# Six tile buffers, earlier token sums and later residual adds in a two-layer spectral and dense kernel

## The chip, the cores and the metric

The kernel runs on one core of one Trainium2 chip, as one launch. The metric is the device time of the whole launch in microseconds (us), the median of several runs.

The engines are named as in the profile: PE is TensorE (matmul), DVE is VectorE, ACT is ScalarE, POOL is GpSimd, and SP is the queue that issues most DMAs. Each engine works through its own list of instructions in order; a wait at the head of a list holds everything behind it.

## What is computed

The input x has 2048 tokens of 1024 features. Two kinds of layer follow each other, twice:

```
x = x + A(layernorm(x))      # A: 2-D real FFT, times a complex filter, inverse FFT
x = x + B(layernorm(x))      # B: Mish(x @ w1 + b1) @ w2,  w1 1024x3584, w2 3584x1024
x = x + A(layernorm(x))
x = x + B(layernorm(x))
```

Both A layers share their filter and both B layers share w1, b1 and w2. The change concerns the two B layers only.

## The kernel before

A B layer handles the 2048 tokens as four chunks of 512 (chunk 0 to 3), each of four tiles of 128 tokens. A tile j (0 to 15) is a 128 x 1024 slice of the resident array XS. The steps of one B layer, in the order in which `layer_B` writes them:

1. **First chunks.** Tiles 0 to 7 get statistics, scale and `apply` (line 521, normalises a tile into a buffer XN), are transposed on PE (line 1108) and copied by DVE (line 1113) into XT. `mm1` (line 1141) multiplies six groups of w1 columns directly. `residual(j)` (line 1284) adds the staged result of the A layer to XS for tiles 4 to 15; the adds for tiles 8 to 11 stand ahead of the normalisation of tiles 6 and 7. Statistics of tiles 8 to 15 come later.
2. **First quads.** `quads` multiplies the remaining eight column groups for chunks 0 and 1 together, in a Strassen-Winograd form of seven products (`product`, line 1177) of four matmuls each per group. It needs sums of the transposed tokens. `open_pair` makes them with four DVE subtractions of 128 x 2048 (line 1156): T1, T2, T4 in three tiles TS0 to TS2 at 128 to 140 KB, and T3 over a part of XT. The first sum reads both chunks. `quads` calls `open_pair` before its first product.
3. **Second product.** Loop n = 0 to 15: `mm2` (line 1228, 28 matmuls of 128 x 512 over all of the hidden features) makes half of the output of one of tiles 0 to 7. It uses PSUM banks 3, 4, 5 in turn, and DVE adds the bank to XS (line 1240). n below 8 makes the first halves, n from 8 the second. In the same loop, for n below 8, `apply(8 + n)` normalises a tile of chunk 2 or 3 into one of two XN buffers, and `turned` issues eight DMA transposes (line 250) from it, all on SP. A buffer is used again two tiles later, when its eight transposes have landed. In the first B layer each `mm2` is followed on DVE by statistics of its half, and from n = 8 also by the scale and `apply` of the finished tile for the next layer: a tail of ten instructions.
4. **Second quads.** `quads` runs over all 14 column groups for chunks 2 and 3, with its own `open_pair` first. Its first group of products is A11 B11, S2 T2, S1 T1, A12 B21, S3 T3, in that order on PE. DVE adds the result of S2 T2 (`add(u2, ...)`, line 1182) before S3 T3 may go into the same bank, then adds S3 T3 (`add(u3, ...)`).
5. **Last second product.** 16 calls of `mm2` for tiles 8 to 15.

The order on every engine is the order of the code. The list of DVE in step 3, for one n, is `apply` of tile 8 + n, then the add of product n. PE can run ahead of the adds by three products, one in each bank.

Of the kernel before, what the change touches and what calls it, by code (L numbers as in the profile page):

```python
# [180 lines left out]
class KB:  # L181
# [183 lines left out]
    def layout(self):  # L365
        K = 1024
        self.o = dict(XR=0, Z=0, X=12 * K, T=20 * K, YK=28 * K, V=40 * K, JT=48 * K, M0=49 * K, IDF=49 * K + 256, RT=50 * K,
                      JUNK=51 * K, WR=54 * K, YS=96 * K, UT=64 * K, MN=64 * K, Y=96 * K, XN=128 * K, U=128 * K,
                      FT=140 * K, BT=144 * K + 512, WT=self.W1_OFF)
        self.ob = dict(AT0=0, AT1=36 * K, XT1=28 * K, XT0=120 * K, W2=64 * K, JUNK=54 * K, SUMS=92 * K, TS=128 * K, XN2=140 * K,  # L370
                       WS=self.arena_bytes - 21 * K)
        assert 149 * K <= self.W1_OFF and 144 * K <= self.ob["WS"], (149 * K, self.W1_OFF)

# [714 lines left out]
    def layer_B(self, li, last):  # L1088
# [60 lines left out]
        def open_pair():  # L1149

            T = [self.alloc(f"TS{i}", self.ob["TS"] + 4096 * i, [4, 512], F16) for i in range(3)]
            lo, hi = [[XT[c].ap[:, 4 * k:4 * k + 4, :] for c in range(2)] for k in range(2)]
            t3 = lo[1].bitcast(F16)
            both = r_xt[0] + r_xt[1]
            tt = lambda dst, x, y, reads, writes: self.op(
                dve, lambda e: e.tensor_tensor(dst, x, y, ALU.subtract), reads=reads, writes=writes)  # L1156
            tt(T[0].ap, lo[1], lo[0], both, [T[0].res])
            tt(T[1].ap, hi[1], T[0].ap, both + [T[0].res], [T[1].res])
            tt(T[2].ap, hi[0], T[1].ap, both + [T[1].res], [T[2].res])
            tt(t3, hi[1], lo[1], r_xt[0], r_xt[1])  # L1160
            return {"B11": (lo[0], r_xt[0]), "B21": (hi[0], r_xt[0]), "B22": (hi[1], r_xt[1]), "T3": (t3, r_xt[1]),
                    "T1": (T[0].ap, [T[0].res]), "T2": (T[1].ap, [T[1].res]), "T4": (T[2].ap, [T[2].res])}

        def open_sums():

            off = self.ob["SUMS"]
            return [self.alloc(f"SUM{i}", off + 2048 * i, [512], F32) for i in range(5)]

        def quads(fgs, slot_of, after=lambda n: None):

            B, sums = open_pair(), open_sums()

            def product(n, bank, a, b, start):
                s = slot_of[n]
                A = self.wblock(s, a)
                mov, res = B[b]
                self.group([lambda e, db=db: e.matmul(PS[:, bank, :], A[:, db, :], mov[:, db, :], start=(start and db == 0), stop=(db == 3),  # L1177
                                                      skip_group_check=True)
                            for db in range(4)], reads=[s.res, s.rs] + list(res), writes=[self.r_bank[bank]])

            def add(dst, bank, x):
                self.op(dve, lambda e: e.tensor_tensor(dst.ap, PS[:, bank, :], x.ap, ALU.add), reads=[self.r_bank[bank], x.res],  # L1182
                        writes=[dst.res])

            def mish(c, ft, src, res):
                at, ra = AT[c], r_at[c][ft]
                self.op(act, lambda e: e.activation(at.ap[:, ft, :], src, ACT.Mish, bias=self.B1[:, ft:ft + 1]),  # L1187
                        reads=[res, self.r_b1], writes=[ra])

            def parts(n):  # L1190
                a, b, d = (3 * (n % 2) + i for i in range(3))
                return a, b, d, sums[n % 2], sums[2 + n % 2], sums[4], 2 * fgs[n]

            N = len(fgs)
            for n in range(N + 1):
                if n < N:
                    a, b, d, p1, u2, u3, ft = parts(n)
                    product(n, a, "A11", "B11", True)
                    self.copy(act, p1.ap, PS[:, a, :], [self.r_bank[a]], [p1.res])
                    product(n, b, "S2", "T2", True)  # L1200
                    add(u2, b, p1)
                if n:
                    _, pb, pd, q1, q2, q3, pft = parts(n - 1)
                    mish(1, pft + 1, q3.ap, q3.res)
                    product(n - 1, pb, "A22", "T4", False)
                    add(q1, pb, q1)
                    mish(0, pft + 1, q1.ap, q1.res)
                    product(n - 1, pd, "S4", "B22", False)
                    add(q2, pd, q2)
                    mish(1, pft, q2.ap, q2.res)  # L1210
                    after(n - 1)
                if n < N:
                    product(n, d, "S1", "T1", True)
                    product(n, a, "A12", "B21", False)
                    mish(0, ft, PS[:, a, :], self.r_bank[a])
                    product(n, b, "S3", "T3", False)
                    add(u3, b, p1)
                    add(u3, d, u3)

        def mm2(c, t, h):  # L1220
            at, ra = AT[c % 2], r_at[c % 2]
            j = 4 * c + t
            bank = 3 + no[0] % 3
            no[0] += 1
            fns = []
            summed = not last and (j, h) == (15, 1)
            for i, ft in enumerate(range(NF)):
                fns.append(lambda e, i=i, ft=ft: e.matmul(  # L1228
                    PS[:, bank, :], at.ap[:, ft, t * P:(t + 1) * P], W2[h][ft // 4].ap[:, ft % 4, :],
                    start=(i == 0), stop=(i == NF - 1 and not summed)))  # L1230

            for lo, hi in ((0, 20), (20, NF)):
                self.group(fns[lo:hi], reads=ra[lo:hi] + [b.res for b in W2[h][lo // 4:hi // 4]], writes=[self.r_bank[bank]])
            if summed:
                self.group([lambda e: e.matmul(PS[:, bank, :], self.IDENT[:], self.XS[:, j, 512:1024], start=False, stop=True)],
                           reads=[self.r_xs[j], self.r_ident], writes=[self.r_bank[bank]])
                self.finish_last(bank)
                return
            xs = self.XS[:, j, h * 512:(h + 1) * 512]
            self.op(dve, lambda e: e.tensor_tensor(xs, PS[:, bank, :], xs, ALU.add),  # L1240
                    reads=[self.r_bank[bank]], writes=[self.r_xs[j]])
            if not last:
                self.stats_half(j, h)
            if h == 0:
                return
            if last:
                self.dma(sp, self.out[0, j * P:(j + 1) * P, :], self.XS[:, j, :], "st", reads=[self.r_xs[j]])
            else:
                if j < 14:
                    self.scales(j, 1)  # L1250
                else:
                    self.root(j, 1)
                self.xn_store(j, self.apply(j, out=True))

        w2v = self.w2.rearrange("(ft fp) d -> fp ft d", fp=P)
        W2 = [[None] * 7, [None] * 7]
# [26 lines left out]
        def residual(j):  # L1283
            self.op(dve, lambda e: e.tensor_tensor(self.XS[:, j, :], self.XS[:, j, :], YS.ap[:, j - 4, :], ALU.add),
                    reads=[YS.res], writes=[self.r_xs[j]])
# [47 lines left out]
        mm1(0, 4)  # L1333
        at_tiles(1)
        mm1(0, 5, mid=turns(1, 0, 1))
        for j in range(8, 12):
            residual(j)
        self.sums_to_mv(6, 2)
        self.scales(6, 2)
        for j in (6, 7):  # L1340
# [7 lines left out]
            mm1(1, fg, 1)  # L1348
        for fg in range(2, 6):
            mm1(1, fg)  # L1350
            residual(10 + fg)
        ws = self.open_slots("WS", self.ob["WS"], 3)
        for n in range(3):
            self.fill_slot(ws[n], 9 + n)
        order = early + [ws[n % 3] for n in range(5)]

        def after(n):
            if n in (3, 4):
                self.fill_slot(order[n + 3], 9 + n)
            if 2 <= n < 6:  # L1360
                for i in range(2 * n - 4, min(2 * n - 2, 7)):
                    load_w2(0, i)
        quads(list(range(6, 14)), order, after)
        for i in range(7):
            load_w2(1, i)
        order = [ws[(n + 2) % 3] for n in range(14)]
        for n in range(3):
            self.fill_slot(order[n], n)
        self.xn_buf = [self.alloc(f"XN{i}", self.ob["XN2"] + i * 2048, [self.D]) for i in range(2)]
        for t in range(8):  # L1370
            self.stats_dve(8 + t)
        self.scales(8, 8)
        for n in range(16):
            if n < 8:
                b = self.apply(8 + n)
                turned(2 + n // 4, n % 4, b)
            t = n % 8
            mm2(t // 4, t % 4, n // 8)

        def after(n):  # L1380
            if n + 3 < 14:
                self.fill_slot(order[n + 3], n + 3)
        quads(list(range(14)), order, after)
        for i in range(7):
            load_w2(1, i)
        if not last:
# [55 lines left out]
```

## Time and profile before

| what | us |
|---|---|
| median of 3 runs | 1049.34 (1048.93 to 1050.88) |
| the profiled execution | 1048.6 |
| its span, first to last instruction | 1046.8 |
| PE busy | 940.1 (90% of the span) |
| DVE busy | 507.3 (48%) |
| ACT busy | 377.8 (36%) |
| POOL busy | 155.9 (15%) |

The mean granted TensorE clock is 0.969 of full. In the profile, busy time of an engine is a mean over very different stages; the waits of PE, and what ended each of them, tell more. The first B layer's step 3 lies at 234 to 355 us, and the second B layer's at 742 to 857 us.

### The profile page before, as it was taken

Reading aid. Unit: us, or ns where it says so; the run is one execution under the profiler, and the core shown is the slowest. Engines: PE = TensorE matmul, PEld = TensorE weight load, DVE = VectorE, ACT = ScalarE, POOL = GpSimd, SP = SyncE. Lnnn points to the kernel's source line nnn. Section 1 sums busy time; section 2 is a strip of 40 time slices with the busy share of each in tenths; the row PEclk is TensorE's granted clock in tenths of the full one; section 3 lists DMA queues with packets and bytes.
Section 4 is the critical chain, followed back from the end, with each engine's and each line's share of the span. In section 5 each row is a group of like instructions: output and inputs, shape, how many; then the busy total and the mean of one; then the engine's idle time right before and its main releaser. Section 6 shows DMA issues by size and latency. Waiting matters only on the chain. (4 is left out here: it accounts for less than half of the span.)

```text
span 1046.8 us, 13594 instructions
## 1 busy us (share of the span) xinstructions
PE 940.1 (90%) x5572; PEld 493.0 (47%) x5650; DVE 507.3 (48%) x915; ACT 377.8 (36%) x531; POOL 155.9 (15%) x184
## 2 busy tenths in 40 slices
PE   1798788999789899999998987999996999999998
PEld 0666655444233344444446757644442434444443
DVE  6797574555216555524436855735701135551111
ACT  7897553550000055510008956645200005551000
POOL 4830054333200050000521200000000000000000
PEclk9999899999889899999999998999998999999999
DMA  9969733367212145340751885335521123434000
GB/s 276 297 188 314 187 132 117 125 211 246 94 26 62 41 164 178 106 166 31 203 103 45 233 207 140 109 123 187 209 70 25 26 84 122 160 106 141 31 21 30
DMA packets 143598, 139.62 MB, mean 133 GB/s; under 512 B 74464, under 2 KB 124464, under 8 KB 143536
## 3 DMA queue, kind: packets, MB, share of 16 engines
q1 hardware_dynamic: 130432, 98.41, 31.7%
q0 software_dynamic: 10928, 38.69, 11.3%
q10 hardware_dynamic: 2176, 1.66, 0.5%
q8 instruction: 44, 0.72, 0.3%
q14 instruction: 18, 0.15, 0.0%
HBM read 100.64 MB, written 33.55 MB: 128 GB/s over the span
## 5 line engine op out<-in xcount | busy, mean ns | idle before, releaser
L1228 PE MATMUL PS<-ARENA 128*128 128x512 bf16 x1756 | 401.6, 389 | 28.1 <-DVE XS L1240 25.8
L1228 PEld LDWEIGHTS PS<-ARENA 128*128 128x128 bf16 x1792 | 178.0, 100 | 251.3 <-DVE XS L1240 31.0
L1177 PE MATMUL PS<-ARENA 128*128 128x512 f16 (+1 forms) x1210 | 270.7, 383 | 13.2 <-DVE ARENA L1156 7.5
L1182 DVE TENSOR_TENSOR ARENA<-PS,ARENA 128x512 f32<-128x512 f32 x220 | 152.1, 692 | 117.1 <-PE PS L1177 115.5
L1177 PEld LDWEIGHTS PS<-ARENA 128*128 128x128 bf16 x1232 | 120.6, 99 | 162.7 <-DVE ARENA L1156 8.4
L577 ACT ACTIVATE ARENA<-PS 128x512 f32<-128x512 f32 (+2 forms) x66 | 51.8, 784 | 289.4 <-PE PS L1177 278.4
L1240 DVE TENSOR_TENSOR XS<-PS,XS 128x512 bf16<-128x512 f32 x63 | 43.2, 689 | 186.7 <-PE PS L1228 186.7
L1187 ACT ACTIVATE ARENA<-ARENA,B 128x512 bf16<-128x512 f32 x132 | 95.2, 721 | 60.4 <-DVE ARENA L1182 54.1
L1141 PE MATMUL PS<-ARENA 128*128 128x256 bf16 (+1 forms) x570 | 89.8, 316 | 0.4
L1084 POOL TENSOR_TENSOR ARENA<-ARENA 128x512 bf16<-128x512 bf16 x56 | 66.5, 1188 | 127.2 <-DMA ARENA<-in_B_w_dram 123.4
L521 DVE TENSOR_SCALAR ARENA<-XS,MV,RS 128x1024 bf16<-128x1024 bf16 x39 | 23.5, 619 | 110.3 <-DMA ARENA<-ARENA 109.6
L1141 PEld LDWEIGHTS PS<-ARENA 128*128 128x128 bf16 x576 | 56.8, 100 | 28.4 <-issue 2.2
L469 DVE BATCH_NORM_STATS2 BN<-XS 128x6 f32<-128x512 bf16 x99 | 63.8, 673 | 6.1 <-DMA XS<-in_A_x_dram 5.1
L1145 ACT ACTIVATE ARENA<-PS,B 128x256 bf16<-128x256 f32 (+1 forms) x72 | 38.3, 541 | 47.9 <-PE PS L1141 47.4
L1187 ACT ACTIVATE ARENA<-PS,B 128x512 bf16<-128x512 f32 x44 | 30.2, 687 | 30.6 <-PE PS L1177 30.6
L441 ACT ACTIVATE RS<-MV,EPS 128x2 f32<-128x2 f32 (+2 forms) x5 | 1.5, 298 | 95.6 <-DVE MV L472 83.7
L802 PE MATMUL PS<-ARENA 128*128 128x256 bf16 x256 | 32.4, 273 | 3.7 <-DVE ARENA L791 3.2
L780 ACT ACTIVATE ARENA<-PS 128x1024 bf16<-128x1024 f32 x32 | 33.4, 1074 | 4.5 <-PE PS L776 4.5
L728 PE MATMUL PS<-FD,ARENA 128*128 128x256 bf16 (+1 forms) x256 | 31.8, 271 | 2.4 <-DVE ARENA L646 1.3
L1156 DVE TENSOR_TENSOR ARENA<-ARENA 128x2048 f16<-128x2048 bf16 x16 | 19.9, 1241 | 25.0 <-PE PS L1141 24.6
L784 DVE TENSOR_TENSOR ARENA<-ARENA 128x1024 bf16<-128x1024 bf16 x32 | 22.0, 688 | 19.8 <-ACT ARENA L780 14.1
L813 ACT ACTIVATE ARENA<-PS 128x1024 bf16<-128x1024 f32 x28 | 29.9, 1092 | 3.7 <-PE PS L802 3.7
(95 smaller groups left out, 692.6 us busy)
## 6 DMA issues: line engine op xcount, KB each, us to landing
ARENA<-in_B_w_dram SPq DMA_DIRECT2D x68, 512.0 KB, 6.6
ARENA<-w1s_scratch SPq DMA_DIRECT2D x30, 896.0 KB, 4.6
w1s_scratch<-ARENA POOLq DMA_DIRECT2D x14, 896.0 KB, 4.1
u_scratch<-ARENA SPq DMA_DIRECT2D x14, 512.0 KB, 3.5
ARENA<-u_scratch SPq DMA_DIRECT2D x14, 512.0 KB, 5.9
w_scratch<-ARENA POOLq DMA_DIRECT2D x8, 512.0 KB, 6.5
ARENA<-w_scratch POOLq DMA_DIRECT2D x8, 512.0 KB, 5.2
out_dram<-XS SPq DMA_DIRECT2D x16, 256.0 KB, 2.0
```

The costliest lines, as they stand in the source:

```text
L469: self.op(self.dve, lambda e: e.bn_stats(self.BN[:, j, 6 * h:6 * h + 6], self.XS[:, j, 512 * h:512 * h + 512]), reads=[self.r_xs[j]], part ...
L577: fn = (lambda e: e.activation(dst, src, ACT.Copy)) if scale is None else \
L780: self.op(act, lambda e: e.activation(x.ap.rearrange("p a b -> p (a b)"), ps, ACT.Copy, scale=SIG), reads=banks, writes=[x.res])
L802: fns.append(lambda e, c=c, part=part: e.matmul(ps[:, c * 256:(c + 1) * 256], yk.ap[:, part, c * P:(c + 1) * P], t[:, (128, 0)[part]:(384, ...
L1084: self.op(self.pool, lambda e, dst=A(dst), x=A(x), y=A(y), op=op: e.tensor_tensor(dst, x, y, op), reads=[b.res], writes=[b.rs])
L1141: fns.append(lambda e, db=db, bank=bank, fl=fl: e.matmul(PS[:, bank, 0:w], wb.ap[:, db, fl * P:(fl + 1) * P], x.ap[:, db, tok], start=(db ...
L1145: self.op(act, lambda e, bank=bank, ft=ft: e.activation(at.ap[:, ft, tok], PS[:, bank, 0:w], ACT.Mish, bias=self.B1[:, ft:ft + 1]), reads= ...
L1177: self.group([lambda e, db=db: e.matmul(PS[:, bank, :], A[:, db, :], mov[:, db, :], start=(start and db == 0), stop=(db == 3), skip_group_ ...
L1182: self.op(dve, lambda e: e.tensor_tensor(dst.ap, PS[:, bank, :], x.ap, ALU.add), reads=[self.r_bank[bank], x.res], writes=[dst.res])
L1187: self.op(act, lambda e: e.activation(at.ap[:, ft, :], src, ACT.Mish, bias=self.B1[:, ft:ft + 1]), reads=[res, self.r_b1], writes=[ra])
L1228: fns.append(lambda e, i=i, ft=ft: e.matmul(PS[:, bank, :], at.ap[:, ft, t * P:(t + 1) * P], W2[h][ft // 4].ap[:, ft % 4, :], start=(i == ...
L1240: self.op(dve, lambda e: e.tensor_tensor(xs, PS[:, bank, :], xs, ALU.add), reads=[self.r_bank[bank]], writes=[self.r_xs[j]])
```

## The change

It has three parts. (a) The buffers of the normalised tiles 8 to 15 are six instead of two, placed where the token sums TS lie. (b) The second `open_pair` stands in the loop of step 3, after the product n = 12, instead of after n = 15. (c) The residual adds of tiles 8 to 11 leave their place ahead of the normalisation of tiles 6 and 7, and all of tiles 8 to 15 are added two at a time beside `mm1` of groups 2 to 5.

```diff
-        self.ob = dict(AT0=0, ... TS=128 * K, XN2=140 * K,
+        self.ob = dict(AT0=0, ... TS=128 * K,
...
-        def quads(fgs, slot_of, after=lambda n: None):
+        def quads(fgs, slot_of, B, after=lambda n: None):
-            B, sums = open_pair(), open_sums()
+            sums = open_sums()
...
         mm1(0, 5, mid=turns(1, 0, 1))
-        for j in range(8, 12):
-            residual(j)
         self.sums_to_mv(6, 2)
...
         for fg in range(2, 6):
             mm1(1, fg)
-            residual(10 + fg)
+            for j in (2 * fg + 4, 2 * fg + 5):
+                residual(j)
...
-        quads(list(range(6, 14)), order, after)
+        quads(list(range(6, 14)), order, open_pair(), after)
...
-        self.xn_buf = [self.alloc(f"XN{i}", self.ob["XN2"] + i * 2048, [self.D]) for i in range(2)]
+        self.xn_buf = [self.alloc(f"XN{i}", self.ob["TS"] + i * 2048, [self.D]) for i in range(6)]
...
             mm2(t // 4, t % 4, n // 8)
+            if n == 12:
+                B = open_pair()
...
-        quads(list(range(14)), order, after)
+        quads(list(range(14)), order, B, after)
```

In the order of instructions only DVE's list differs. L1240 is the add of a product, L1156 are the four token sums, L1182 are the adds of the quads, L469 is a half of a tile's statistics, L507 is the last step of its scale, L521 normalises it.

DVE in the first B layer, where step 3 ends and step 4 begins, before:

```order
L507 SCALAR_TENSOR_TENSOR RS<-RS 128x1
L521 TENSOR_SCALAR FD<-XS,MV,RS 128x1024
L1156 TENSOR_TENSOR ARENA<-ARENA 128x2048 x4
L1182 TENSOR_TENSOR ARENA<-PS,ARENA 128x512 x70
L1240 TENSOR_TENSOR XS<-PS,XS 128x512
```

The same sums of the first B layer on DVE, now:

```order
L507 SCALAR_TENSOR_TENSOR RS<-RS 128x1
L521 TENSOR_SCALAR FD<-XS,MV,RS 128x1024
L1156 TENSOR_TENSOR ARENA<-ARENA 128x2048 x4
L1240 TENSOR_TENSOR XS<-PS,XS 128x512
L469 BN_STATS BN<-XS 128x6
```

The sums stood between the tail of n = 15 and the first add of the quads; they stand between the tail of n = 12 and the add of n = 13, so three whole tails (L1240 to L521) lie between the sums and the quads.

DVE at the same place of the second B layer, where a tail is the add alone, as a difference of the two lists:

```order
 L521 TENSOR_SCALAR ARENA<-XS,MV,RS 128x1024
-L1240 TENSOR_TENSOR XS<-PS,XS 128x512 x9
+L1240 TENSOR_TENSOR XS<-PS,XS 128x512 x6
 L1156 TENSOR_TENSOR ARENA<-ARENA 128x2048 x4
+L1240 TENSOR_TENSOR XS<-PS,XS 128x512 x3
 L1182 TENSOR_TENSOR ARENA<-PS,ARENA 128x512 x70
```

Three of the nine adds behind the last `apply` moved from ahead of the sums to behind them.

DVE in step 1 of a B layer, around the normalisation of tiles 6 and 7, as a difference (L1113 copies transposed tiles, L1284 is a residual add, L461 begins the scale of tiles 6 and 7):

```order
 L521 TENSOR_SCALAR ARENA<-XS,MV,RS 128x1024 x2
 L1113 COPY ARENA<-PS 128x8x128 x2
-L1284 TENSOR_TENSOR XS<-XS,ARENA 128x1024 x4
 L461 TENSOR_SCALAR MV<-BN 128x4
 L462 TENSOR_TENSOR RS<-MV 128x2
```

The four adds left this place; they stand behind the copies of tiles 6 and 7, where there are now eight in a row.

## Rows read from the trace of the kernel before

**Rows 1.** Waits of PE, whole span: line, releaser, us in total, times, longest.

```profile
PE PS L1228 <- DVE XS L1240: 25.8, 10, 4.8
PE PS L1177 <- DVE ARENA L1156: 7.5, 2, 5.1
```

**Rows 2.** Timeline of PE, first B layer: start us, us, line, tile, xcount [idle before].

```profile
234.15 36.42 PE L1228 MATMUL PS<-ARENA 128*128 128x512 bf16 x165
275.36 3.60 PE L1228 MATMUL PS<-ARENA 128*128 128x512 bf16 x8 [4.79 <-DVE XS L1240]
...
354.88 1.03 PE L1177 MATMUL PS<-ARENA 128*128 128x512 bf16 x4
361.05 4.38 PE L1177 MATMUL PS<-ARENA 128*128 128x512 f16 x10 [5.14 <-DVE ARENA L1156]
```

**Rows 3.** Timeline of DVE, first B layer, the same stretch.

```profile
262.08 1.51 DVE L521 TENSOR_SCALAR ARENA<-XS,MV,RS 128x1024 bf16<-128x1024 bf16 x1 [10.55 <-DMA ARENA<-ARENA]
...
355.07 0.69 DVE L1240 TENSOR_TENSOR XS<-PS,XS 128x512 bf16<-128x512 f32 x1 [2.53 <-PE PS L1228]
...
358.51 4.99 DVE L1156 TENSOR_TENSOR ARENA<-ARENA 128x2048 f16<-128x2048 bf16 x4
363.42 0.68 DVE L1182 TENSOR_TENSOR ARENA<-PS,ARENA 128x512 f32<-128x512 f32 x1
366.76 1.42 DVE L1182 TENSOR_TENSOR ARENA<-PS,ARENA 128x512 f32<-128x512 f32 x2 [2.65 <-PE PS L1177]
```

**Rows 4.** Timeline of the SP queue, first B layer.

```profile
248.57 87.60 SPq L250 DMA_TRANSPOSE ARENA<-ARENA  x64
```

**Rows 5.** Timeline of PE, second B layer.

```profile
742.04 36.42 PE L1228 MATMUL PS<-ARENA 128*128 128x512 bf16 x165
...
856.97 1.03 PE L1177 MATMUL PS<-ARENA 128*128 128x512 bf16 x4
860.31 9.97 PE L1177 MATMUL PS<-ARENA 128*128 128x512 f16 x37 [2.31 <-DVE ARENA L1156]
```

**Rows 6.** Timeline of DVE, second B layer.

```profile
819.95 1.88 DVE L1240 TENSOR_TENSOR XS<-PS,XS 128x512 bf16<-128x512 f32 x3
...
857.77 4.99 DVE L1156 TENSOR_TENSOR ARENA<-ARENA 128x2048 f16<-128x2048 bf16 x4
862.68 0.68 DVE L1182 TENSOR_TENSOR ARENA<-PS,ARENA 128x512 f32<-128x512 f32 x1
865.57 1.42 DVE L1182 TENSOR_TENSOR ARENA<-PS,ARENA 128x512 f32<-128x512 f32 x2 [2.20 <-PE PS L1177]
```

**Rows 7.** Timeline of the SP queue, second B layer.

```profile
756.35 82.34 SPq L250 DMA_TRANSPOSE ARENA<-ARENA  x64
```

**Rows 8.** The chain that ended last: the landing behind a sixth tile's last transpose.

```profile
817.06 2.33 DMA ARENA<-ARENA
```

**Rows 9.** Stretches of PE: us, busy (instructions), granted clock, DMA share, GB/s.

```profile
361.00:363.00 2.00, 1.96 (x5) 0.50 0.00 0
```

**Rows 10.** Stretches of all engines: us, PE, PEld, DVE, ACT, POOL busy, clock, DMA share, GB/s.

```profile
789.00:795.00 6.00, 5.45 (x13) 1.94 (x14) 0.50 (x1) 0.00 (x0) 0.00 (x0) 0.50 0.13 27
```

**Rows 11.** Timeline of DVE, step 1 of the first, then of the second B layer.

```profile
154.39 5.66 DVE L1284 TENSOR_TENSOR XS<-XS,ARENA 128x1024 bf16<-128x1024 bf16 x4
...
162.14 1.00 DVE L521 TENSOR_SCALAR ARENA<-XS,MV,RS 128x1024 bf16<-128x1024 bf16 x2
...
668.24 2.49 DVE L1284 TENSOR_TENSOR XS<-XS,ARENA 128x1024 bf16<-128x1024 bf16 x4
```

**Rows 12.** Timeline of PE and of POOL in step 1 of the B layers.

```profile
162.75 1.08 PE L1108 MATMUL PS<-IDENT,ARENA 128*128 128x128 bf16 x16 [2.98 <-DVE ARENA L521]
...
673.42 1.08 PE L1108 MATMUL PS<-IDENT,ARENA 128*128 128x128 bf16 x16 [1.63 <-DVE ARENA L521]
...
153.66 5.85 POOL L1084 TENSOR_TENSOR ARENA<-ARENA 128x512 bf16<-128x512 bf16 x4
```

**Rows 13.** Stretch of step 1 behind that wait, all engines, columns as in rows 10.

```profile
162.70:168.00 5.30, 5.25 (x41) 4.18 (x42) 5.04 (x8) 0.95 (x2) 0.00 (x0) 0.68 0.07 25
```

More of the change, by code (lines that the diff above doesn't have):

```diff
@@ L369, in layout @@
                       FT=140 * K, BT=144 * K + 512, WT=self.W1_OFF)
-        self.ob = dict(AT0=0, AT1=36 * K, XT1=28 * K, XT0=120 * K, W2=64 * K, JUNK=54 * K, SUMS=92 * K, TS=128 * K, XN2=140 * K,
+        self.ob = dict(AT0=0, AT1=36 * K, XT1=28 * K, XT0=120 * K, W2=64 * K, JUNK=54 * K, SUMS=92 * K, TS=128 * K,
                        WS=self.arena_bytes - 21 * K)
```

## The prediction

> **What bounds the kernel now.** PE is busy 90% of the span, so I read first what PE waits for, then the stretch around each wait, engine by engine. Two of its waits belong to the change: 25.8 us in front of `mm2` for the add of an earlier product, and 7.5 us in front of the second quads for the token sums [rows 1]. Both lie in steps 3 and 4 of each B layer.
>
> How the first arises: PE's first six `mm2` run without a pause, 36.42 us or 6.07 us each [rows 2, 5]. Then PE stops for 4.79 us [rows 2], because the add it needs sits on DVE behind an `apply` that has waited up to 10.55 us for a buffer's transposes to land [rows 3]. With two buffers, DVE moves at SP's pace. SP spends 87.60 us issuing the 64 transposes in the first B layer and 82.34 us in the second [rows 4, 7], about 10.3 us a tile against 6.07 us a product.
>
> [...]
>
> Unhindered, 16 products take 97.1 us. Step 3 would end at 234.15 + 97.1 = 331.3 instead of 354.88, and at 742.04 + 97.1 = 839.1 instead of 856.97 [rows 2, 5]. So the stalls, with the clock, cost 23.6 and 17.9 us.
>
> **The change part by part.**
>
> (a) *Six buffers.* No instruction is added. `apply` for n = 0 to 5 has a buffer at once; for n = 6 it needs tile 0's transposes, landed at 262.08 in the first layer [rows 3], while product 5 ends near 234.15 + 36.4 = 270.6. For n = 7 tile 1 landed about 274 against product 6 near 276.6. I therefore put the PE stalls at zero and step 3 on PE at 331.3 and 839.1. The new place, over the token sums, adds a wait for the first quads' last reads; those are over before DVE's last quad adds, which stand ahead anyway: nothing.
>
> What is late next: the transposes. SP was already issuing without a gap, so more buffers do not hasten it. The last issue ends at 248.57 + 87.60 = 336.2 and 756.35 + 82.34 = 838.7 [rows 4, 7]; the landing takes 2.33 us more [rows 8]: 338.5 and 841.0. That is later than the end of step 3 on PE in both layers (331.3, 839.1).
>
> [...]
>
> (b) *Sums after n = 12.* The four sums read both chunks, so on DVE they wait for the last landing, 338.5, though they stand earlier. Meanwhile adds 13 to 15 are held behind them. PE can still fill its three banks, so step 3 on PE is not delayed; the price falls on the quads.
>
> First B layer: sums run 338.5 to 343.5 (4.99 us [rows 3]), the second done at 341.0. Then three tails; one lasts 358.51 − 355.07 = 3.44 us [rows 3], three 10.3, to 353.8. Then `add(u2)`, 0.68 us [rows 3], to 354.5. PE runs A11 B11 to 332.2, idles until 341.0, runs S2 T2, S1 T1, A12 B21 at the lower clock (12 x 0.43 = 5.2 us) to 346.2, and idles again until 354.5, since S3 T3 goes into the bank that `add(u2)` reads. S3 T3 at the lower clock, 1.7 us, ends at 356.2. In the trace of before, DVE starts on that result at 366.76 [rows 3]: 10.5 us earlier. PE restarts cold: before, 361.05 to 366.76 for 16 matmuls is 2.25 us over full clock and ends warm. The lower level lasts some 4.5 us (that loss doubled) to 6 us [rows 10]; 1.7 of it is counted, so the remaining 2.8 to 4.3 us cost half, 1.4 to 2.2. Net 8.3 to 9.1; I take **8.7**.
>
> Second B layer: tails are adds alone. Sums 841.0 to 846.0, the second at 843.5; three adds 1.88 [rows 6] to 847.9; `add(u2)` to 848.6. PE: A11 B11 to 840.0, idle to 843.5, three products at the lower clock to 848.7, S3 T3 in 0.9 to 1.7 us, to 849.6 or 850.4. Before: 865.57 [rows 6]. Gain 15.2 to 16.0, less up to 0.7 for a clock that is low a little longer: **15.3**.
>
> So part (b) by itself loses here. With the sums left behind n = 15, the tails would be done by some 335, `add(u2)` would end near 344.2, and S3 T3 near 348 in the first layer. What pays is (a).
>
> (c) *Residual adds.* The four adds ahead of tiles 6 and 7 leave the path. Second layer: 2.49 us go [rows 11], and PE waits 1.63 us there [rows 12], so **1.6**. First layer: they take 5.66 us, 2.3 times as long, because POOL's w1 sums run at 153.66 to 159.5 [rows 11, 12]. PE's wait is 2.98 us [rows 12]. Without the adds, the eleven small steps of the scale and the first `apply` (154.39 + 5.66 = 160.05 to 162.7, 2.6 us) start at 154.4, beside POOL. Stretched like the adds, the 5.1 us to 159.5 do 2.2 us of that work, and the rest ends at 159.9, about when PE comes free (162.75 − 2.98 = 159.8): 2.8 us won. If the small steps stretch more, say fourfold, 1.3 us of work are left at 159.5, and 1.9 us are won. Behind the wait the clock was 0.68 for 5.3 us [rows 13], 5.3 x 0.32 = 1.7 us lost; a short wait may spare that. Together 1.9 to 4.5, and I take **3.5**. The eight adds behind take 2.49 x 2, with DVE idle ahead of the quads; the cover is the 20 us of `mm1` that follow. Nothing.
>
> [...]
>
> **Sum.** 8.7 + 15.3 + 1.6 + 3.5 = 29.1 us. Against the profiled execution: 1048.6 − 29.1 = 1019.5 us (1.8 of it lies outside the span). The median before is 0.7 higher than that execution: **1020.2 us**.
>
> **The rivals.**
>
> 1. *The buffers free the transposes.* If SP's 1.23 us an issue were back-pressure and fell, PE would run through both steps: step 3 ends at 331.3 and 839.1, and S3 T3 some 20 matmuls (4.3 us) later, at 335.6 and 843.4, which is 31.2 and 22.2 us earlier than before. With (c), 58.5: 991 us. Against it: SP's issues were gapless with two buffers. 3%.
> 2. *The held tails cost more.* If in the first layer the tails also wait on one another (the next layer's tiles use two buffers, stored by POOL) and the low clock lasts on, that layer gives 0 to 5 us and (c) is swallowed by a later wait: 15 to 22 us, 1027 to 1034. For it: two idle spells of PE in a row, 8.8 and 8.3 us, of a kind that the trace does not hold. 13%.
> 3. *Slower.* With no work left to pace them, 64 queued transposes collide with the w2 and w1 loads and SP slows down. All of S2 T2 to S3 T3 hangs on the last landing, so the change loses when it is later by 29.1 / 2 = 14.6 us in each layer: 1.50 us an issue instead of 1.28. At 1.6, it is 21 us late twice, and the time is 1062. For it: 248.57 to 336.2 is 5 us longer than in the second layer, beside such loads. Against it: the loads are the same and issued before. 3%.
> 4. *Nothing.* The stalls go but return as the wait for the sums, 1047 to 1051. It needs landings some 14 us later, or a wait that I don't see. 2%.
>
> **How the numbers follow.** The forecast, 1020.2, holds 79%. Its own ends: 8.3 to 10.5, 14.5 to 16.0, 1.0 to 1.7 and 1.0 to 4.5 give 24.8 to 32.7 us, or 1016.6 to 1024.5. Errors in the estimated ends of DVE's and PE's work widen it by some 3 us at either side, and the upper end reaches into rival 2: 1013 to 1029. A measurement of this kernel tells about 0.2% from no change. Faster by more: 79 + 3 + 13 = 95%; within: 2%; slower: 3%.
>
> **What would show it.** In the profile after, the wait of `mm2` for the adds (25.8 us) is near zero; SP's 64 transposes still take 82 to 88 us in a row; DVE waits at the sums, not at `apply`, about 22 us in the first layer and 19 in the second; PE waits for the sums about 9 and 3.5 us, and for `add(u2)` about 8 us in the first layer alone; the wait at 162.75 has shrunk below 1.5 us. Wrong it would be if SP's issues shorten or lengthen, if PE still waits inside step 3, or if the quads start with no wait for `add(u2)`.

## The result and the profile after

| | before | changed |
|---|---|---|
| median, us | 1050.11 (4 runs) | 1018.47 (4 runs: 1016.51 to 1020.55) |
| profiled execution, us | 1048.6 | 1016.51 |
| its span, us | 1046.8 | 1014.7 |
| PE busy, us | 940.1 | 925.4 |
| mean granted clock | 0.969 | 0.980 |

The ratio is 0.9691, 95% interval 0.9652 to 0.973: the kernel is 31.6 us faster. The forecast was 1020.2, in a range of 1013 to 1029. Single executions of one kernel differ by up to 9 us here (the kernel before took 1044.3 to 1053.1 us in one set of seven), so differences of a few us are read from the traces below, and the medians only have to agree with them.

The waits of PE in the changed kernel, whole span (line, releaser, us in total, times, longest), answer to [rows 1]:

```profile
PE PS L1177 <- DVE ARENA L1156: 12.6, 2, 8.8
PE PS L1177 <- DVE ARENA L1182: 11.8, 6, 8.1
```

The wait of `mm2` (L1228) for the adds, 25.8 us before, has left the list. The wait for the token sums has grown from 7.5 to 12.6 us, and a wait for `add(u2)`, 8.1 us at its longest, is new.

The timeline of PE in the first B layer, against [rows 2]:

```profile
228.67 96.86 PE L1228 MATMUL PS<-ARENA 128*128 128x512 bf16 x439
325.36 1.03 PE L1177 MATMUL PS<-ARENA 128*128 128x512 bf16 x4
335.15 5.30 PE L1177 MATMUL PS<-ARENA 128*128 128x512 f16 x12 [8.77 <-DVE ARENA L1156]
348.55 15.84 PE L1177 MATMUL PS<-ARENA 128*128 128x512 f16 x59 [8.09 <-DVE ARENA L1182]
```

All sixteen products run in one piece of 96.86 us (97.1 forecast). Then PE makes A11 B11, stands 8.77 us for the sums, makes three products, and stands 8.09 us again.

The timeline of DVE at the same place, against [rows 3]:

```profile
307.43 0.69 DVE L1240 TENSOR_TENSOR XS<-PS,XS 128x512 bf16<-128x512 f32 x1 [2.53 <-PE PS L1228]
...
332.61 5.00 DVE L1156 TENSOR_TENSOR ARENA<-ARENA 128x2048 f16<-128x2048 bf16 x4 [21.66 <-DMA ARENA<-ARENA]
337.53 0.68 DVE L1240 TENSOR_TENSOR XS<-PS,XS 128x512 bf16<-128x512 f32 x1
...
340.96 0.68 DVE L1240 TENSOR_TENSOR XS<-PS,XS 128x512 bf16<-128x512 f32 x1
...
344.38 0.68 DVE L1240 TENSOR_TENSOR XS<-PS,XS 128x512 bf16<-128x512 f32 x1
...
347.81 0.68 DVE L1182 TENSOR_TENSOR ARENA<-PS,ARENA 128x512 f32<-128x512 f32 x1
350.47 1.42 DVE L1182 TENSOR_TENSOR ARENA<-PS,ARENA 128x512 f32<-128x512 f32 x2 [1.98 <-PE PS L1177]
```

DVE comes to the sums after product 12 and stands there 21.66 us for the transposes. Behind the sums, three tails follow at 3.43 us each (337.53, 340.96, 344.38), and only then `add(u2)`.

The SP queue in the two B layers, against [rows 4, 7], has not changed its pace:

```profile
243.73 87.67 SPq L250 DMA_TRANSPOSE ARENA<-ARENA  x64
...
740.21 83.53 SPq L250 DMA_TRANSPOSE ARENA<-ARENA  x64
```

PE in the second B layer, against [rows 5]:

```profile
725.89 96.86 PE L1228 MATMUL PS<-ARENA 128*128 128x512 bf16 x439
822.59 1.03 PE L1177 MATMUL PS<-ARENA 128*128 128x512 bf16 x4
827.49 4.33 PE L1177 MATMUL PS<-ARENA 128*128 128x512 f16 x12 [3.87 <-DVE ARENA L1156]
832.40 37.95 PE L1177 MATMUL PS<-ARENA 128*128 128x512 f16 x172 [0.59 <-DVE ARENA L1182]
```

DVE there, at `add(u3)`, against the last line of [rows 6]:

```profile
833.48 1.42 DVE L1182 TENSOR_TENSOR ARENA<-PS,ARENA 128x512 f32<-128x512 f32 x2 [1.13 <-PE PS L1177]
```

Where the 32.1 us of span went is read by how much earlier the same instruction starts than before. A difference between two such places is what the stretch between them gave:

| place | before, us | changed, us | earlier by | gained since |
|---|---|---|---|---|
| transposes of tile 4 on PE (L1108), ahead of any edit | 151.83 | 151.07 | 0.8 | 0.8 |
| first `mm2`, first B layer | 234.15 | 228.67 | 5.5 | 4.7 (c) |
| add of the second quad group, PE in full pace again | 372.80 | 358.38 | 14.4 | 8.9 (a, b) |
| first `mm2`, second B layer | 742.04 | 725.89 | 16.2 | 1.7 (c) |
| `add(u3)` of the first quad group, second B layer | 865.57 | 833.48 | 32.1 | 15.9 (a, b) |

The third place on DVE, before and then changed (granted clock 1.00 over 372 to 378 and over 358 to 364 us):

```profile
372.80 1.42 DVE L1182 TENSOR_TENSOR ARENA<-PS,ARENA 128x512 f32<-128x512 f32 x2 [1.90 <-PE PS L1177]
...
358.38 1.42 DVE L1182 TENSOR_TENSOR ARENA<-PS,ARENA 128x512 f32<-128x512 f32 x2 [1.90 <-PE PS L1177]
```

### The profile page after: what moved, and what is told of

Read it like the earlier page. It is cut to its first block, busy times and chain, and to the rows that moved or that the text cites. A ratio compares the mean times of both kernels' runs of the same rounds, so it can differ in the third digit from the quotient of the medians.

```text
span 1014.7 us, 13594 instructions
## 1 busy us (share of the span) xinstructions
PE 925.4 (91%) x5572; PEld 489.6 (48%) x5650; DVE 508.5 (50%) x915; ACT 377.6 (37%) x531; POOL 156.5 (15%) x184
## 5 line engine op out<-in xcount | busy, mean ns | idle before, releaser
L1228 PE MATMUL PS<-ARENA 128*128 128x512 bf16 x1756 | 385.6, 379 | 1.9
L1177 PE MATMUL PS<-ARENA 128*128 128x512 f16 (+1 forms) x1210 | 274.1, 386 | 26.6 <-DVE ARENA L1156 12.6
L1228 PEld LDWEIGHTS PS<-ARENA 128*128 128x128 bf16 x1792 | 175.2, 98 | 211.8 <-DVE ARENA L1182 0.8
L1182 DVE TENSOR_TENSOR ARENA<-PS,ARENA 128x512 f32<-128x512 f32 x220 | 152.2, 692 | 116.7 <-PE PS L1177 115.1
L1240 DVE TENSOR_TENSOR XS<-PS,XS 128x512 bf16<-128x512 f32 x63 | 43.3, 690 | 228.5 <-PE PS L1228 228.5
L469 DVE BATCH_NORM_STATS2 BN<-XS 128x6 f32<-128x512 bf16 x99 | 63.8, 673 | 5.3 <-DMA XS<-in_A_x_dram 4.3
L1156 DVE TENSOR_TENSOR ARENA<-ARENA 128x2048 f16<-128x2048 bf16 x16 | 19.8, 1238 | 60.0 <-DMA ARENA<-ARENA 41.3
L1023 PE MATMUL PS<-MT,ARENA 128*128 128x32 bf16 (+1 forms) x512 | 21.7, 200 | 10.3 <-DMA ARENA<-u_scratch 7.0
```

The source lines that it names most:

```text
L469: self.op(self.dve, lambda e: e.bn_stats(self.BN[:, j, 6 * h:6 * h + 6], self.XS[:, j, 512 * h:512 * h + 512]), reads=[self.r_xs[j]], part ...
L1228: fns.append(lambda e, i=i, ft=ft: e.matmul(PS[:, bank, :], at.ap[:, ft, t * P:(t + 1) * P], W2[h][ft // 4].ap[:, ft % 4, :], start=(i == ...
```

## The experiments

All kernels are compared with the kernel before, whose median beside them was 1048.4 to 1050.1 us.

**1. Part (b) undone.** Sums behind all sixteen products, six buffers:

```diff
-            if n == 12:
-                B = open_pair()
-        quads(list(range(14)), order, B, after)
+        quads(list(range(14)), order, open_pair(), after)
```

> The changed kernel with one part undone: the second set of token sums stands again behind all sixteen products; six buffers and late residual adds stay. Theory (the sums wait for the last transposes wherever they stand, and hold DVE's adds behind them): in the first B layer add(u2) no longer waits for three tails of 3.4 us, PE's 8.1 us wait for it goes, and one of two cold restarts; 10 us there, under 1 us in the second layer: 1006 to 1009 us, against 1018.5 for the changed kernel. Rival (early sums are worth the wait for sums that they were meant to remove): 2 to 8 us slower than the changed kernel, 1020 to 1026 us.

Measured: 1005.44 us, ratio 0.9574 (0.9532 to 0.9616). That is 13.0 us faster than the changed kernel by the medians. The timeline of DVE in the first B layer:

```profile
325.99 0.69 DVE L1240 TENSOR_TENSOR XS<-PS,XS 128x512 bf16<-128x512 f32 x1 [2.52 <-PE PS L1228]
333.55 5.00 DVE L1156 TENSOR_TENSOR ARENA<-ARENA 128x2048 f16<-128x2048 bf16 x4 [4.04 <-DMA ARENA<-ARENA]
338.47 0.68 DVE L1182 TENSOR_TENSOR ARENA<-PS,ARENA 128x512 f32<-128x512 f32 x1
...
348.16 1.42 DVE L1182 TENSOR_TENSOR ARENA<-PS,ARENA 128x512 f32<-128x512 f32 x2 [1.90 <-PE PS L1177]
```

The sums start at about the same time, 104.5 us after the first `mm2` (333.55 − 229.10) against 103.9 in the changed kernel (332.61 − 228.67). But here the last tail, which began at 325.99, is already done, and `add(u2)` follows the sums directly. From the first `mm2` to the add of the second quad group it is 119.1 us (348.16) against 129.7; in the second layer, 107.1 to `add(u3)` against 107.6. So 10.6 and 0.5 us by the traces; the rest of the 13.0 us of the medians is within what executions differ by. The rival, that early sums are worth something here, has fallen.

**2. The early sums with two buffers.** Part (a) undone:

```diff
-        self.xn_buf = [self.alloc(f"XN{i}", self.ob["TS"] + i * 2048, [self.D]) for i in range(6)]
+        self.xn_buf = [self.alloc(f"XN{i}", 140 * 1024 + i * 2048, [self.D]) for i in range(2)]
```

> The changed kernel with two buffers again, at the old place; the sums stay after n = 12 and the residual adds stay late. Theory (early sums pay only where PE is late and the transposes land first): step 3 ends as late as before, 24 and 18 us over its work, but the sums run inside it, and the waits of PE for them (5.1 and 2.3 us) and the cold matmuls behind go, some 6.6 and 5.0 us; with 6.5 of the residual adds 1050 - 18 = 1032 us. Rival (early sums cost DVE the same whatever the buffers): 1050 - 6.5 + 10 = 1053 us. Second rival (the sums' place does not matter): 1043.5 us.

Measured: 1034.63 us, ratio 0.9857 (0.982 to 0.9895); 1032 was expected. With this edit and that of experiment 1 together, part (c) is left alone:

> Part (c) alone: two buffers and late sums as before the change, only the residual adds stand late. Theory: 1050 - 6.5 = 1043.5 us, and the three parts then add up as (c) 6.5, (a) some 37, (b) a loss of 11 behind (a). Rival: the time of before.

Measured: 1044.71 us, ratio 0.9955 (0.9935 to 0.9975), so the rival, no gain, lies outside the interval. That is 3.7 us below the kernel before beside it (1048.39), and 6.5 were expected. Its trace is 2.3 us late ahead of any edit (tile 4 on PE at 154.15 us against 151.83), and its span is 3.9 us shorter all the same (1042.9 against 1046.8), so by the trace (c) gave 6.2. By the medians, one after the other, (c) gave 3.7 us, (a) another 39.3 (1044.71 to 1005.44; some 37 expected), and (b) took 13.0 of it back (11 expected).

The same move of the sums therefore gains 10 us with two buffers (1044.7 to 1034.6) and loses 13 with six (1005.4 to 1018.5). DVE with two buffers and early sums, first B layer:

```profile
331.80 0.69 DVE L1240 TENSOR_TENSOR XS<-PS,XS 128x512 bf16<-128x512 f32 x1 [2.52 <-PE PS L1228]
335.24 5.00 DVE L1156 TENSOR_TENSOR ARENA<-ARENA 128x2048 f16<-128x2048 bf16 x4
340.15 0.68 DVE L1240 TENSOR_TENSOR XS<-PS,XS 128x512 bf16<-128x512 f32 x1
```

The sums have no idle time ahead of them. PE is so late, stalled 31.0 us by the adds in the two layers together, that the transposes have landed when DVE comes to the sums, and there is time for the tails.

**3. The bound itself.** If SP's issues set the landing, taking two of the eight tiles off SP should free the quads. Here PE transposes the last two:

```diff
                 b = self.apply(8 + n)
-                turned(2 + n // 4, n % 4, b)
+                xn[8 + n] = b
+                if n < 6:
+                    turned(2 + n // 4, n % 4, b)
...
             mm2(t // 4, t % 4, n // 8)
+            if n in (7, 8):
+                transposed(3, n - 5, xn[n + 7])
```

> The changed kernel, where the last two of the eight tiles are transposed by PE behind products 7 and 8 and copied by DVE, instead of by SP's sixteen last DMA transposes. Theory (SP's issue of 1.28 us each sets when the quads may start): SP ends 20 us earlier, before product 12's add, the sums run inside step 3, and PE has no wait for them and none over 1 us for add(u2); PE pays 1.1 us a layer for the transposes. Gain some 20 us in the first and 5 us in the second B layer: 993 us. Rival (the landing is set by something other than the issues, or the held tails cost as much again): 1010 to 1020 us.

Measured: 994.03 us, ratio 0.9468 (0.9429 to 0.9506), and in a second set

> The version with the last two tiles transposed by PE, once more, beside the next two: 992 to 996 us.

992.33 us, ratio 0.9461 (0.9436 to 0.9486). This is the fastest version: 24 to 26 us below the changed kernel, and close to the 991 us that rival 1 of the prediction gave for a PE that runs through both steps. PE in its first B layer (first set):

```profile
230.15 48.51 PE L1228 MATMUL PS<-ARENA 128*128 128x512 bf16 x224
278.50 0.61 PE L1108 MATMUL PS<-IDENT,ARENA 128*128 128x128 bf16 x8
278.95 6.21 PE L1228 MATMUL PS<-ARENA 128*128 128x512 bf16 x28
...
327.74 3.62 PE L1177 MATMUL PS<-ARENA 128*128 128x512 bf16 x16
332.11 13.12 PE L1177 MATMUL PS<-ARENA 128*128 128x512 f16 x60 [0.76 <-DVE ARENA L1182]
```

The SP queue there, and the sums on DVE:

```profile
245.20 65.67 SPq L250 DMA_TRANSPOSE ARENA<-ARENA  x48
...
313.24 4.99 DVE L1156 TENSOR_TENSOR ARENA<-ARENA 128x2048 f16<-128x2048 bf16 x4
```

SP ends at 310.9, while DVE works on the tail of product 12 (309.81 to 313.3), and the sums follow that tail with no wait. The first four products of the quads run in one piece (x16) behind the last `mm2`, and 0.76 us is all that is left of the two waits. A transposed tile costs PE 0.45 us (278.50 to 278.95, where the next product starts).

**4. The place of the sums once the transposes are early.** Experiment 3 with the sums behind all sixteen products:

> The same with the token sums behind all sixteen products instead of behind product 12. Theory (part (b) pays when the transposes have landed before DVE comes to the sums): the waits of before come back, 5.1 us and 2.3 us of PE, with 2.3 and 1.8 us of cold matmuls behind: 11.5 us slower, 1005.5 us. Rival (the place of the sums costs as with six buffers alone, where late sums were 13 us better): at or under 994 us.

Measured: 1002.95 us, ratio 0.9567 (0.9542 to 0.9592), 10.6 us above the same version with early sums in the same set. PE's waits for the sums are those of before, to the tenth [rows 1]:

```profile
PE PS L1177 <- DVE ARENA L1156: 7.5, 2, 5.1
```

So the early sums are right again as soon as the transposes are early. The other way round, two tiles on PE are worth little while the sums are late: this version is only 2.5 us below experiment 1 (1005.44), whose interval overlaps with its own. Moving the tiles gained 24 to 26 us with early sums. The two edits pay together.

**5. All tiles on PE.** No DMA transposes in the B layers:

```diff
-                b = self.apply(8 + n)
-                turned(2 + n // 4, n % 4, b)
+                xn[8 + n] = self.apply(8 + n)
...
+            if 2 <= n < 10:
+                transposed(2 + (n - 2) // 4, (n - 2) % 4, xn[n + 6])
```

> All eight tiles transposed by PE, each two products after its normalisation, and no DMA transposes in the B layers; sums after product 12. Theory (a tile on PE costs its eight matmuls, 0.45 us net in the trace, and one copy on DVE that has time): 12 tiles more in two layers, 5.4 us above the version with two tiles: 999 us. Rival (PE waits for the tiles, or the adds come late behind DVE's copies): 1003 us or more. If it is under 994, the DMA transposes cost PE something that the trace does not name.

Measured: 997.58 us, ratio 0.9509 (0.9488 to 0.9529): 5.3 us above the version with two tiles, as twelve more tiles at 0.45 us say. The DMA transposes save PE that much, and no further cost of theirs to PE shows at this precision.

**6. How many buffers.** Sums behind all sixteen products, four buffers, then three (`range(4)`, `range(3)`), beside the changed kernel once more:

> The changed kernel itself, unaltered, timed beside the next three on the same chip: 1016 to 1021 us.

> Four buffers instead of six, and the token sums behind all sixteen products, as in the run that undid part (b) alone. Theory (what counts is that the add of product n is done before product n + 3 starts, three banks later): by the landings of before, n = 4 to 7 wait for tiles 0 to 3, landed near 262, 274, 285 and 295 us, and products 7 to 10 would start near 277, 283, 289 and 295: no PE wait but some half microsecond at product 10. The time is that of six buffers with late sums, 1005 to 1008 us. Rival (each wait of DVE for a buffer costs PE): 5 us or more above it.

> Three buffers, and the token sums behind all sixteen products. Theory: now n = 3 to 7 wait for tiles 0 to 4; product 8 waits for the add of 5 behind tile 2 (286 against 283 us), and from there each product follows a landing 10.2 us after the last: step 3 ends some 10 us later than unhindered in the first B layer and 7 in the second, the sums are no longer late, and S3 T3 follows some 4.5 and 3 us later than with six buffers: 1011 to 1015 us. Rival (a third buffer is enough, since PE has three banks): 1005 to 1007 us.

Measured: the changed kernel 1018.67 us, ratio 0.9701 (0.9661 to 0.9742); four buffers 1005.48, ratio 0.9587 (0.9542 to 0.9633); three 1025.34, ratio 0.9764 (0.9721 to 0.9807). Four are as good as six. With four, DVE still waits for buffers (waits of DVE, whole span):

```profile
DVE ARENA L521 <- DMA ARENA<-ARENA: 51.3, 8, 9.0
```

PE hardly does; this is the one break in its step 3 of the first B layer, and there is none in the second:

```profile
292.13 36.43 PE L1228 MATMUL PS<-ARENA 128*128 128x512 bf16 x165 [1.46 <-DVE XS L1240]
```

The three products that PE can run ahead cover DVE's waits, but for one of 1.46 us. With three buffers they don't; PE in the first B layer:

```profile
281.42 6.22 PE L1228 MATMUL PS<-ARENA 128*128 128x512 bf16 x27 [3.18 <-DVE XS L1240]
291.60 8.79 PE L1228 MATMUL PS<-ARENA 128*128 128x512 bf16 x27 [3.96 <-DVE XS L1240]
```

The expectation for three buffers, 1011 to 1015, was too low. By the trace the add of S3 T3 comes 7.0 us later behind the first `mm2` than with six buffers and late sums, in both layers (4.5 and 3 expected). Step 3 ends 11.6 and 9.9 us later than sixteen products in one piece (10 and 7 expected); PE, late again, then waits 5.14 and 2.31 us for the sums, and its matmuls are slower behind the first of these waits, as before (71 in 17.58 us, 0.248 each; before, 55 in 14.31 us, 0.260 each; without a pause 0.217, from 36.42 us for six products). This makes about 1019.5, and the profiled execution took 1020.47; the other three of that kernel took 1024.7 to 1028.2, which the one trace doesn't explain. That remains open.

**7. The residual adds back in their old places**, the rest as changed:

```diff
+        for j in range(8, 12):
+            residual(j)
         self.sums_to_mv(6, 2)
...
-            for j in (2 * fg + 4, 2 * fg + 5):
-                residual(j)
+            residual(10 + fg)
```

> The changed kernel with the residual adds back in their old places; buffers and sums stay changed. Theory (their move is worth what the traces show between step 1 and step 2, 4.7 us in the first and 1.8 us in the second B layer): 1025 us, 6.5 above the changed kernel. Rival (the moved adds only shorten a wait that a later one swallows, and the gain is noise of the early part): 1017 to 1020 us.

Measured: 1024.68 us, ratio 0.9754 (0.9714 to 0.9795): 6.2 us above the changed kernel. PE's wait ahead of tiles 6 and 7 is back to the hundredth, with the slow matmuls behind it:

```profile
163.02 1.08 PE L1108 MATMUL PS<-IDENT,ARENA 128*128 128x128 bf16 x16 [2.98 <-DVE ARENA L521]
163.93 20.01 PE L1141 MATMUL PS<-ARENA 128*128 128x256 bf16 x104
```

In the changed kernel the same two groups read:

```profile
159.24 1.08 PE L1108 MATMUL PS<-IDENT,ARENA 128*128 128x128 bf16 x16 [0.22 <-DVE ARENA L521]
160.15 18.57 PE L1141 MATMUL PS<-ARENA 128*128 128x256 bf16 x102
```

## Why the prediction held

The time, 1018.5, lies 1.7 us under the forecast of 1020.2. The gain is further off, 31.6 us by the medians and 32.1 by the spans, where 29.1 were forecast. The times came closer by chance: the median before is 1050.11 with its fourth run, 0.8 us above the one that the forecast started from. Of the 3.0 us by which the span gained more, 0.8 lie ahead of any edit, 1.3 in the stretches of the residual adds, and 0.9 in the waits and cold matmuls between step 3 and the quads. Step by step:

- *Stalls of step 3 to zero.* Right: one piece of 96.86 us in both layers, and no wait of PE for an add of `mm2`.
- *The transposes become the bound, at SP's pace.* Right: 87.67 and 83.53 us in a row. Experiment 3 shows the series on SP as the cause, not only in place: with a quarter of it gone, the waits behind go, and 24 to 26 us with them. What no run separates is whether 1.23 us is SP's own work or the pace at which the transposes are taken from it. For the first speaks that the DMA engines were busy for 10.7% of 320 to 333 us, and that a transpose landed 2.4 us (median) after its issue began; but that is argued.
- *The landing.* Two small errors cancel, which is luck. I added 2.33 us to the end of the last issue; the chain of the changed kernel counts it from the start of that issue, 1.2 us less:

```profile
822.50 2.32 DMA ARENA<-ARENA
...
824.95 1.24 DVE ARENA L1156
```

  Against that, the issues began 0.6 us later behind step 3's start in the first layer (15.1 against 14.4 us), and took 1.2 us longer in the second (83.53 against 82.34). The sums began 103.9 and 99.1 us after the first `mm2`; 104.4 and 99.0 were forecast.
- *The three tails ahead of `add(u2)`.* Right: PE's second wait is 8.09 us (about 8 forecast), and S3 T3 was done 121.8 us after the first `mm2` (122.0 forecast). The verdict that (b) by itself loses here stands: 13 us by the medians, 11.1 by the traces (experiment 1). The other waits came as forecast too: DVE stood 21.66 and 19.60 us at the sums (22 and 19 forecast), PE 8.77 and 3.87 (9 and 3.5).
- *The cold matmuls*, those at the lower clock. The 0.43 us of a matmul in that sum is in no row as such: [rows 10] have 13 in 5.45 us at a granted clock of 0.50, 0.42 each, where six products of 28 in one piece took 36.42 us [rows 2], 0.217 each. The 12 matmuls behind the first wait took 5.30 us, 0.44 each, at a granted 0.50 over 335 to 340 us (5.2 forecast); in the second layer 4.33, at a mean clock of 0.66 over 827 to 832 us, so that term was some 0.9 us too dear. The net gains, 8.9 and 15.9 us, compare with 8.7 and 15.3. Stretches of PE in the two layers, columns as in [rows 9]:

```profile
335.00:340.00 5.00, 4.84 (x12) 0.50 0.00 0
...
827.00:832.00 5.00, 4.33 (x12) 0.66 0.36 139
```

- *The residual adds.* The mis-sized term: 4.7 and 1.7 us instead of 3.5 and 1.6. Of the first, 2.76 us are the wait (2.98 to 0.22) and 1.44 the matmuls behind it (20.01 to 18.57), which now keep the full clock (1.00 over 159.2 to 164.5 us, against 0.68 in [rows 13]); I had counted both only in part. The other 0.5 us is a wait of PE for POOL in the first quads, 1.16 us before and 0.63 now. It was 0.89 in experiment 1, where the residual adds stand late as well, so it isn't shown to belong to (c). The steps of the scale did stretch, as the adds had (5.66 against 2.49 us, [rows 11]): POOL's sums ran from 152.91 to 157.79 us, and three of the eleven steps took 1.00 us each beside them. In the second B layer, where POOL ran nothing at that place, the same three took 0.16 or 0.17. One of them, first in the first layer and then in the second:

```profile
154.34 1.00 DVE L463 TENSOR_TENSOR MV<-MV,RS 128x2 f32<-128x2 f32 x1
...
654.28 0.16 DVE L463 TENSOR_TENSOR MV<-MV,RS 128x2 f32<-128x2 f32 x1
```

  The steps ended in time all the same: the first `apply` began at 158.63, and PE, free at 159.02, had its tile at 159.24.
- 0.8 us of the gain lies ahead of any edit and is a difference between executions.

Of the rivals, the first (faster transposes) and the third (slower ones) are excluded by SP's rows. The second, a dearer backlog of tails, did not come about: the tails kept 3.43 us each, and none waited on another. The fourth, no gain, is excluded by the 31.6 us.

## What to carry to other kernels

Give a stalled stage more buffers only as far as the engines' own slack needs (here three products of PSUM banks; four buffers did what six did), and look at once for the series that is next: 64 issues in a row on one queue were the new bound, and moving a quarter of them to another engine was worth 24 to 26 us more, nearly as much again as the whole change, though only 2.5 while the sums stood late. Place an instruction early in an in-order list only if its input is there when the list reaches it. Where it was not, the sums held everything behind them on DVE (for 21.66 us, first B layer of the changed kernel): the same move gained 10 us, lost 13 and gained 11, according to when the transposes landed.

## What the runs showed of the hardware

A DMA transpose of a 128 x 128 block took 1.23 us of issue on the SP queue (median, in the kernel before as in the changed one); eight of them, a tile, landed 10.2 us apart with three buffers (DVE's `apply` at 270.04, 280.21 and 290.39), and the same tile took PE 0.45 us net and DVE one copy (0.68 us for tile 4 in the changed kernel). The slower route was still the better one for six tiles of eight (992.3 against 997.6 us, where 999 was expected).

What a stop of PE cost the matmuls behind it could not be read here from its length alone. Behind waits of 3.96 us, 28 matmuls took 9.04 us in one place (the kernel before, second B layer; granted clock 0.50 over 789 to 795 us) and 6.22 us in another (two buffers and early sums, first B layer; 0.222 us each, where the piece without a pause has 0.217):

```profile
789.55 9.04 PE L1228 MATMUL PS<-ARENA 128*128 128x512 bf16 x28 [3.96 <-DVE XS L1240]
...
293.09 6.22 PE L1228 MATMUL PS<-ARENA 128*128 128x512 bf16 x28 [3.96 <-DVE XS L1240]
```
